# Query features in an attention-and-experts kernel: from turned exponentials to a second, transposed projection

## The chip, the cores and the metric

The kernel runs on one core of one Trainium2 chip. The metric is the device time of one execution in microseconds (us), shown as the median of several runs. Beside it stands the profile of one execution, whose span is the time from the first to the last instruction on the core.

## The reference

Two stages follow each other. The first is linear attention with random features over 4 batches, 8 heads, 576 positions and 64 channels, with 128 features:

```
def phi(x):
    proj = np.einsum('bhsd,md->bhsm', x, omega)
    sq = np.sum(x * x, axis=-1, keepdims=True) / 2.0
    h = proj - sq
    h = h - np.max(h, axis=-1, keepdims=True)
    return np.exp(h) / np.sqrt(m)
q_p, k_p = phi(q * scale), phi(k * scale)
kv = np.einsum('bhsm,bhsd->bhmd', k_p, v)
z = np.sum(k_p, axis=2)
num = np.einsum('bhsm,bhmd->bhsd', q_p, kv)
den = np.einsum('bhsm,bhm->bhs', q_p, z)[..., None] + 1e-06
out = num / den
```

The second takes the 2304 tokens of 512 channels through 8 experts (hidden size 1024, relu), each expert's result weighted by a gate that is normalized eight times over rows and columns, and adds them up.

## The kernel before

**The attention** is cut into 36 jobs, 18 for keys and 18 for queries. A job is 128 positions (or two times 64 left over) of eight head-and-position groups. The list `jobs` begins with keys, then alternates keys and queries, and ends with queries alone. A function `tick(j)` writes out, for every j, what is done for job j (`now`), for the job before it (`prev` in the new code, `job(j - 1)` in the old), for `job(j - 2)` and for the job two ahead (`far`). The order of the instructions of each engine is fixed as written (they are pinned), so an engine that waits holds up everything written behind it.

A job goes through these steps. `transposes` (L442, tile `tp`) turns the inputs with four matmuls against the identity; `transposed_copy` brings them to SBUF as `th`, by ScalarE for keys (L450) and by VectorE for queries (L452). `projections` (L462, tile `pp`) multiplies by `omega`, eight matmuls into two PSUM banks; each takes 64 rows of the array, the bank of g = 0 the upper rows and that of g = 1 the lower ones, and each f32 matmul stands as two records in the trace. `maxima` (L472) takes the largest feature of each position. `shifts` adds the three parts of the shift (L477, tile `cn`) and adds it to the first bank (L479, tile `ex`). `exps` takes the exponential: of the first bank in one instruction (L488), of the second in four, with the shift as bias (L492).

For a key job, `keys_by_values` (L499, tile `kv`) multiplies the features by the values. For a query job, the next tick's `query_transposes` (L559, tile `qp`) turns the eight 128x128 blocks of features with TensorE, `query_copy` (L566, tile `qt`) brings them to SBUF by ScalarE, and a tick later `numerators` (L583, tile `np`) multiplies them by the key-value sums; `quotients` (L598 to L602) divides, and `token_transposes` (L618, tile `xp`) turns the tokens for the experts.

Six PSUM banks are shared by `pp`, `tp`, `qp`, `np`, `xp` and the gate's logits (`lp`, L194); two more hold the key-value sums. Between the steps of the attention, generators advance the experts' preparation: the tokens of three chunks are added and subtracted in pairs by GpSimd (L116), rounded by ScalarE (L120), their low parts taken by VectorE or GpSimd (L125), and the pieces are written to DRAM (`xd`) from four buffers (`xs`). Behind the attention TensorE runs the experts in fp32r, in pieces of 384 columns (L730) and 256 columns (L854), in an order made by a planner.

Of the kernel before, what the change touches and what calls it, by code (L numbers as in the profile page):

```python
# [9 lines left out]
F32 = mybir.dt.float32  # L10
F32R = mybir.dt.float32r
AF = mybir.ActivationFunctionType
ALU = mybir.AluOpType
AX = mybir.AxisListType


def raw(ap):

    return ap.bitcast(F32)
# [3 lines left out]
def moe_attention_kernel(  # L23
# [23 lines left out]
    nc = tc.nc  # L47
    B, H, S, D = q.shape
# [4 lines left out]
    P = 128  # L53
# [26 lines left out]
    def bank(name):  # L80
        return ps[0].tile([P, 512], F32, tag="b", name=name)


    ident = const.tile([P, P], F32, name="ident")
# [238 lines left out]
    sc = sc_cm.__enter__()  # L323
# [4 lines left out]
    sc.tile([P, 1, D], F32, name="om2")  # L328
    oms = sc.tile([P, 2, D], F32, name="oms")
    omt = sc.tile([P, M], F32, name="omt")  # L330

    def busy(n):

        wp_ = bank("warm")
        for i in range(n):
            nc.tensor.transpose(wp_[:, i % 4 * P : (i % 4 + 1) * P], ident, ident)

    def prepare_omega():

        nc.scalar.mul(oms, om.to_broadcast([P, 2, D]), 1.0 / math.sqrt(math.sqrt(D)))  # L340
        om_ps = bank("om_ps")
        nc.tensor.transpose(om_ps[:, :P], oms.rearrange("p a d -> p (a d)"), ident)
        nc.scalar.copy(omt, om_ps[:, :M])

    GC = P // KD
    wgs = sc.tile([P, KD, GC], F32, name="wgs")
# [82 lines left out]
    def slots(key, hh, g):  # L429

        if key[0] == "r":
            return [(2 * i + g, 0) for i in range(4)]
        return [(4 * hh + i, g) for i in range(4)]
# [11 lines left out]
    def transposed_copy(jb):  # L445

        which, tp = jb[0], tps.pop(jb)
        th = sc.tile([P, 4, P], F32, tag="th", bufs=2, name="th")
        if which == "k":
            nc.scalar.copy(th.rearrange("p a s -> p (a s)"), tp)  # L450
        else:
            nc.vector.tensor_copy(th.rearrange("p a s -> p (a s)"), tp)  # L452
        ths[jb] = th

    def projections(jb):

        th = ths.pop(jb)
        pp = [bank("pp") for _ in range(2)]
        for i in range(4):
            for g in range(2):  # L460
                r = slice(g * D, (g + 1) * D)
                nc.tensor.matmul(pp[g][:, i * M : (i + 1) * M], lhsT=th[r, i], rhs=omt[r], start=True, stop=True)  # L462
        p3s[jb] = [p.rearrange("p (h m) -> p h m", h=4) for p in pp]

    def shift_of(jb):

        which, key, hh = jb[:3]
        return sqt[which, key].rearrange("p h j t -> p (h j) t")[:, 8 * hh : 8 * hh + 8]

    def maxima(jb, g):  # L470

        nc.vector.tensor_reduce(shift_of(jb)[:, g::2, 1], p3s[jb][g], axis=AX.X, op=ALU.max, negate=True)  # L472

    def shifts(jb):

        cn = sc.tile([P, 8], F32, tag="cn", bufs=4, name="cn")
        nc.vector.tensor_reduce(cn, shift_of(jb), axis=AX.X, op=ALU.add)  # L477
        ex = [sc.tile([P, 4, M], F32, tag="ex", bufs=6, name="ex") for _ in range(2)]
        nc.vector.tensor_tensor(  # L479
            ex[0], p3s[jb][0], cn[:, 0::2].unsqueeze(2).to_broadcast([P, 4, M]), op=ALU.add  # L480
        )
        cns[jb], exs[jb] = cn, ex

    def exps(jb, g):

        ex = exs[jb][g]
        if g == 0:
            nc.scalar.activation(ex, ex, AF.Exp)  # L488
            return
        c4 = cns.pop(jb)[:, 1::2]  # L490
        for i in range(4):
            nc.scalar.activation(ex[:, i, :], p3s[jb][1][:, i, :], AF.Exp, bias=c4[:, i : i + 1])  # L492

    tps, ths, p3s, cns, exs, qts, nums = {}, {}, {}, {}, {}, {}, {}

    def kv_mm(b, h, r, ex, rhs, z, start, stop):

# [51 lines left out]
    closing = []  # L549
    xts = {}  # L550

    def query_transposes(jb):

        ex = exs.pop(jb)
        tps = []
        for g in (1, 0):
            tp = bank("qp")
            for i in range(4):
                nc.tensor.transpose(tp[:, i * P : (i + 1) * P], ex[g][:, i, :], ident)  # L559
            tps.append((g, tp))  # L560
        return tps

    def query_copy(jb, g, tp):

        t = sc.tile([P, 4, P], F32, tag="qt", bufs=4, name="qt")
        nc.scalar.copy(t.rearrange("p a s -> p (a s)"), tp)  # L566
        qts[jb, g] = t

    def numerators(jb):

        key, hh = jb[1:3]
        shared = key[0] == "r"
        n3s = []
        for g in range(2):
            nps = bank("np")
            n3 = nps[:, : 4 * (D + 1)].rearrange("p (h d) -> p h d", h=4)
            n3s.append(n3)
            qt = qts.pop((jb, g))
            for i, (h, j) in enumerate(slots(key, hh, g)):
                for a in range(2):  # L580
                    r = slice(a * SR, (a + 1) * SR)
                    kv = kvs[2 * key[1] + a if shared else key[0]]
                    nc.tensor.matmul(  # L583
                        n3[r, i, :], lhsT=qt[:, i, r], rhs=kv[:, h], start=True, stop=True
                    )
        nums[jb] = n3s
# [372 lines left out]
    jobs = []  # L959
# [46 lines left out]
    def go_on():  # L1006
        for it in list(extra):
            if next(it, it) is it:
                extra.remove(it)

    def tick(j):

        def job(n, which=None):
            return jobs[n] if 0 <= n < len(jobs) and which in (None, jobs[n][0]) else None

        now, nxt, far = job(j), job(j + 1), job(j + 2)
        if j < 0:
            transposes(nxt)
            transposed_copy(nxt)
            busy(3)  # L1020
            _, w, key = sq_todo.pop(0)
            squares(w, key)
            it = sq_halves.pop(0)
            next(it)
            next(it)
            transposes(far)
            transposed_copy(far)
            ensure_squares(0)
            return
        closed = []  # L1030

        def close():
            while closing:
                closed.append(closing.pop(0))
                kv_copy(*closed[-1])

        close()
        if now:
            projections(now)
            maxima(now, 0)  # L1040
        if j >= 3:
            ensure_squares(j)
        if far:
            transposes(far)
        shared = None
        if job(j - 1, "k") and job(j - 1)[1][0] == "r":
            shared = keys_by_values(job(j - 1))
            next(shared)
            close()
        it = None  # L1050
        if j >= 0 and sq_halves:
            it = sq_halves.pop(0)
            next(it)
        if 1 <= j < 3:
            ensure_squares(j - (j < 2))
        if job(j - 1, "q"):
            for t in query_transposes(job(j - 1)):
                query_copy(job(j - 1), *t)
        if now:
            if not nxt:  # L1060
                go_on()
            maxima(now, 1)
            shifts(now)
        for b, g in closed:
            kv_add(b, g)
        if far:
            transposed_copy(far)
        if now:
            if it:
                next(it)  # L1070
            exps(now, 1)
        go_on()
        for xt, i, t in turned[: 1 if j < 28 else None]:
            turned.pop(0)
            token_copy(token_transposes(xt, i, t), t)
        if now:
            exps(now, 0)
        for it in leftover:
            next(it, None)
        leftover.clear()  # L1080
        if job(j - 2, "q"):
            numerators(job(j - 2))
        if shared:
            leftover.append(shared)
        elif job(j - 1, "k"):
            it = keys_by_values(job(j - 1))
            next(it)
            leftover.append(it)
        if job(j - 2, "q"):
            quotients(job(j - 2))  # L1090
        if nxt:
            go_on()
# [4 lines left out]
    busy(16)  # L1097
    ensure_loads(0)
    prepare_omega()
    for i in range(-1, len(jobs)):  # L1100
        if i == 7:
            stage(0, 1)
            prepare_gate()
        if i == 12:
            it = first_splits()
            next(it)
            extra.append(it)
        if i == 32:
            stage(0, 2)
        tick(i)  # L1110
        ensure_loads(i + 1)
    z = len(jobs)
    numerators(jobs[z - 2])
    for g, tp in query_transposes(jobs[z - 1]):
        query_copy(jobs[z - 1], g, tp)
    go_on()
    xpss = [token_transposes(*it) for it in turned[:2]]
    quotients(jobs[z - 2])
# [5 lines left out]
    xt, i, t = turned.pop(0)  # L1124
# [4 lines left out]
    xt, i, t = turned.pop(0)  # L1129
# [48 lines left out]
    for s, (u, n) in enumerate(steps):  # L1178
        c = n // (CT // 2)
# [27 lines left out]
        for k, i in enumerate(ORDER):  # L1207
# [3 lines left out]
            if k < ((5, 5, 4) if s > 2 else (3, 4, 3))[n % 3] and todo:  # L1211
                pc = todo.pop(0)
                first(*pc)
                j = ORDER.index(pc[2])
# [44 lines left out]
```

## Time and profile before

| what | value |
|---|---|
| median of 3 runs | 1576.74 us (1575.73 to 1577.12) |
| profiled execution, its own time | 1575.99 us |
| its span | 1574.2 us |
| TensorE clock granted | 1.00 of full speed in every slice |
| attention | to about 146.8 us, when the first experts' matmul starts |

The busy time of TensorE is modelled and overlaps from one matmul to the next, so the distance from the start of one group of records to the start of the next says more of what a group costs than its busy time.

### The profile page before, as it was taken

What the parts mean: (1) busy time and instruction counts of PE and PEld (TensorE: products, weight loads), DVE (VectorE), ACT (ScalarE), POOL (GpSimd) and SP (SyncE); (2) the same over time, 40 slices, a digit from 0 to 9 for tenths busy, and PEclk for the clock granted to TensorE, in tenths of its full rate; (3) what the DMA queues carried; (4) which work ended last, traced back from release to release, by engine and by line L of the source; (5) the groups of instructions that cost most, each with busy time, mean ns of one, the idle gap of its engine ahead of it and who ended that gap; (6) DMA issues with size and microseconds to landing.
All of it is one profiled execution on the core that took longest, in us unless ns stands there. A gap on an engine that the chain in (4) does not pass through costs nothing.

```text
span 1574.2 us, 31256 instructions
## 1 busy us (share of the span) xinstructions
PE 1561.7 (99%) x12295; PEld 1535.4 (98%) x12295; DVE 1361.5 (86%) x2573; ACT 766.2 (49%) x1388; POOL 277.1 (18%) x285
## 2 busy tenths in 40 slices
PE   9999999999999999999999999999999999999999
PEld 8887999999999999999999999999999999999998
DVE  7999989898888898888789898889888888989775
ACT  8998654444443444444444443444443444444341
POOL 6665211111010111111011111111110111110000
PEclk9999999999999999999999999999999999999999
DMA  9546866645666666656666666656566666656562
GB/s 227 139 148 259 332 249 223 229 173 214 210 222 215 225 197 216 222 176 216 214 221 212 225 208 212 217 185 225 195 219 212 216 217 208 225 185 212 182 230 92
DMA packets 105730, 330.81 MB, mean 210 GB/s; under 512 B 14704, under 2 KB 43888, under 8 KB 105584
## 3 DMA queue, kind: packets, MB, share of 16 engines
q1 hardware_dynamic: 105296, 328.55, 61.8%
q8 instruction: 98, 1.61, 0.4%
q14 instruction: 48, 0.39, 0.1%
q10 hardware_dynamic: 288, 0.26, 0.0%
HBM read 307.54 MB, written 21.23 MB: 209 GB/s over the span
## 4 chain that ended last, share of the span: by engine, by line
PE 91%; DVE 3%; DMA 3%; ACT 1%; SPq 1%; POOL 1%; issue 0%; DVEq 0%; POOLq 0%; ACTq 0%
PE hx L730 25%; PE x L854 25%; PE hz L730 19%; PE z L854 19%; PE p L938 1%; PE pp L462 1%; DMA xd<-xs 1%; DVE sqs L472 1%; DMA oa<-xd 1%; DMA xs<-xd 1%; DMA k<-in_k_dram 1%; DVE xs L125 0%; PE tp L442 0%; PE np L583 0%; PE kv L499 0%
## 5 line engine op out<-in xcount | busy, mean ns | idle before, releaser
L730 PE MATMUL hx<-xs,wh 128*128 128x384 f32 x1528 | 367.0, 335 | 1.1 <-ACT hn L745 0.8
L730 PE MATMUL hz<-xs,wh 128*128 128x384 f32 x1144 | 282.1, 336 | 0.3 <-DMA xs<-xd 0.3
L730 PEld LDWEIGHTS hx<-xs,wh 128*128 128x128 f32 x1528 | 265.4, 188 | 2.8 <-ACT xs L120 1.4
L235 POOL TENSOR_TENSOR st<-st 128x512 f32<-128x512 f32 x75 | 117.6, 1568 | 613.6 <-DVE wl L269 611.3
L828 ACT ACTIVATE bh<-hr 128x512 fp32r<-128x512 f32 x141 | 89.1, 632 | 237.6 <-PE x L854 230.1
L730 PEld LDWEIGHTS hz<-xs,wh 128*128 128x128 f32 x1144 | 199.8, 188 | 1.5 <-DVE out L888 0.9
L730 PE MATMUL hx<-xs,wl 128*128 128x384 f32 x764 | 200.1, 335 | 0.0
L888 DVE SCALAR_TENSOR_TENSOR out<-x,prob,out 128x256 f32<-128x256 f32 x324 | 153.7, 477 | 52.3 <-PE x L854 50.4
L268 ACT CAST wh<-st 128x512 fp32r<-128x512 f32 x172 | 103.5, 620 | 103.4 <-PE hx L730 52.1
L730 PE MATMUL hz<-xs,wl 128*128 128x384 f32 x572 | 151.8, 335 | 0.0
L825 DVE TENSOR_TENSOR sl<-sm,sh 128x512 fp32r<-128x512 f32 x141 | 112.7, 799 | 44.2 <-ACT sh L823 38.4
L823 ACT CAST sh<-sm 128x512 fp32r<-128x512 f32 x141 | 87.7, 622 | 106.3 <-PE z L854 82.0
L730 PEld LDWEIGHTS hx<-xs,wl 128*128 128x128 f32 x764 | 137.4, 188 | 0.0
L269 DVE TENSOR_TENSOR wl<-st,wh 128x512 fp32r<-128x512 f32 x172 | 123.1, 725 | 9.9 <-ACT wh L268 9.9
L783 DVE SCALAR_TENSOR_TENSOR sm<-hr,sm 128x256 f32<-128x256 f32 x282 | 124.6, 442 | 3.0
L809 ACT CAST sh<-sm 128x512 fp32r<-128x512 f32 x140 | 87.1, 622 | 71.3 <-PE x L854 68.5
L854 PE MATMUL z<-wh,sh 128*128 128x256 f32 x564 | 115.9, 280 | 0.6 <-ACT sh L809 0.5
L854 PE MATMUL x<-wl,sh 128*128 128x256 f32 x564 | 114.5, 280 | 0.0
L854 PE MATMUL z<-wl,sh 128*128 128x256 f32 x564 | 113.9, 280 | 0.0
L854 PE MATMUL x<-wh,sl 128*128 128x256 f32 x564 | 113.6, 279 | 0.0
L791 ACT ACTIVATE ah<-hr 128x256 fp32r<-128x256 f32 x141 | 58.9, 418 | 109.8 <-PE x L854 95.5
L854 PE MATMUL x<-wh,sh 128*128 128x256 f32 x564 | 112.3, 279 | 0.0
(194 smaller groups left out, 3555.6 us busy)
## 6 DMA issues: line engine op xcount, KB each, us to landing
xs<-xd SPq DMA_DIRECT2D x327, 768.0 KB, 4.5
st<-in_moe_w_dram SPq DMA_DIRECT2D x66, 512.0 KB, 4.9
xd<-xs SPq DMA_DIRECT2D x21, 768.0 KB, 5.3
v<-in_v_dram SPq DMA_DIRECT2D x8, 512.0 KB, 7.0
q<-in_q_dram SPq DMA_DIRECT2D x8, 512.0 KB, 7.1
k<-in_k_dram SPq DMA_DIRECT2D x7, 512.0 KB, 7.3
out_dram<-out SPq DMA_DIRECT2D x18, 128.0 KB, 3.9
oa<-xd SPq DMA_DIRECT2D x2, 768.0 KB, 8.9
```

Source lines behind the costliest of these rows:

```text
L235: nc.gpsimd.tensor_tensor(o, a, b, op=op)
L268: nc.scalar.copy(hi, o)
L269: nc.vector.tensor_tensor(lo, o, raw(hi), op=ALU.subtract)
L730: nc.tensor.matmul(pb, lhsT=a[:, k, g * P : (g + 1) * P], rhs=x[:, b, k, :], start=i in (1, 5, 2) and j == 0, stop=j == len(prods) - 1, sk ...
L783: nc.vector.scalar_tensor_tensor(o, in0=a, scalar=0.0, in1=b, op0=ALU.max, op1=op)
L791: nc.scalar.activation(ah, a11, AF.Relu)
L809: nc.scalar.copy(sh, sm)
L823: nc.scalar.copy(sh, sm)
L825: nc.vector.tensor_tensor(sl, sm, raw(sh), op=ALU.subtract)
L828: nc.scalar.activation(bh, a[:, 1:], AF.Relu)
L854: nc.tensor.matmul(pb, lhsT=ops[s][i][a][:, f], rhs=wt[u, 2, i][b][:, f], start=bool(start) and j == 0, stop=j == len(prods) - 1, skip_gro ...
L888: nc.vector.scalar_tensor_tensor(o, in0=pb, scalar=p, in1=o, op0=ALU.mult, op1=ALU.add)
```

## The change

For query jobs the features are no longer turned after the exponential. The projection is computed a second time with the operands exchanged, so that features stand on the partitions and positions along the free axis. The shift, one number for each position, then has to be added along the free axis. For that, `shifts` writes it in two parts into a zeroed 128x128 tile `cnw` (rounded to fp32r, and what the rounding left), `shifts_turned` turns that tile with one matmul against the identity and copies it to `ct`, and `query_features` adds it to the second projection with eight fp32r matmuls against constant tiles `pick` of ones and zeros. `query_exps` takes the exponential straight from PSUM into `qt`. The first projection stays, since the maximum is taken from it; the add to the first bank and the two forms of the exponential fall away for query jobs, and so do the turning and the copy. Buffers: `th` grows from two to four, `qt` shares the six buffers of `ex`, and constants are prepared at the start.

```
+    wide = [sc.tile([P, P], F32R, name=f"cw{i}") for i in range(2)]
+    turnedc = [sc.tile([P, P], F32R, name=f"ct{i}") for i in range(2)]
+    for t in wide:
+        nc.gpsimd.memset(raw(t), 0.0)
...
+    def prepare_pick():
+        for i in range(4):
+            t = sc.tile([P, 1], F32, tag="cn", bufs=4, name="pk")
+            nc.vector.tensor_reduce(t, ident[:, i::32], axis=AX.X, op=ALU.add)
+            nc.vector.tensor_copy(pick[:, i], t.to_broadcast([P, P]))
...
-        th = sc.tile([P, 4, P], F32, tag="th", bufs=2, name="th")
+        th = sc.tile([P, 4, P], F32, tag="th", bufs=4, name="th")
...
 def shifts(jb):
+        if jb[0] == "q":
+            cnw = wide[len(cnws) % 2]
+            cnws.append(cnw)
+            c8 = sc.tile([P, 8], F32, tag="cn", bufs=4, name="cq")
+            nc.vector.tensor_reduce(c8, shift_of(jb), axis=AX.X, op=ALU.add)
+            parts = cnw.rearrange("p (g a c) -> p a c g", g=2, a=2)[:, :, :4, :]
+            c8 = c8.rearrange("p (i g) -> p i g", g=2)
+            nc.vector.tensor_copy(parts[:, 0], c8)
+            nc.vector.tensor_tensor(parts[:, 1], c8, raw(parts[:, 0]), op=ALU.subtract)
+            return
 def exps(jb, g):
+        if jb[0] == "q":
+            return
...
+    def shifts_turned(jb):
+        cp = p3s[jb][0].rearrange("p h m -> p (h m)")[:, :P]
+        nc.tensor.transpose(cp, raw(cnws[-1]), ident)
+        ct = turnedc[len(cnws) % 2]
+        nc.vector.tensor_copy(ct, cp)
...
+    def query_features(jb):
+        th, ct = ths.pop(jb), cts.pop(jb)
+        qp = [bank("qp") for _ in range(2)]
+        rows = [slice(g * D, (g + 1) * D) for g in range(2)]
+        for g, r in enumerate(rows):
+            nc.tensor.matmul(
+                qp[g][:, :], lhsT=omt[r], rhs=th[r].rearrange("p a s -> p (a s)"), start=True, stop=False,
+                skip_group_check=True,
+            )
+        for i in range(4):
+            for g, r in enumerate(rows):
+                nc.tensor.matmul(
+                    qp[g][:, i * P : (i + 1) * P], lhsT=pick[r, i],
+                    rhs=ct[r], start=False, stop=i == 3, skip_group_check=True,
+                )
+    def query_exps(jb):
+        for g, qp in enumerate(qps.pop(jb)):
+            t = sc.tile([P, 4, P], F32, tag="ex", bufs=6, name="qt")
+            nc.scalar.activation(t.rearrange("p a s -> p (a s)"), qp, AF.Exp)
...
 def tick(j):
         close()
+        prev = job(j - 1, "q")
+        if prev:
+            shifts_turned(prev)
         if now:
             projections(now)
...
-        if job(j - 1, "q"):
-            for t in query_transposes(job(j - 1)):
-                query_copy(job(j - 1), *t)
+        if prev:
+            query_features(prev)
...
             exps(now, 1)
+            exps(now, 0)
+        if prev:
+            query_exps(prev)
         go_on()
```

Of the lines left out, the exponential of the first bank moves ahead of the token copies for key jobs too, and the end of the loop does the new steps for the last job.

## Rows read from the trace of the kernel before

**Rows 1.** The page's chain that ended last: shares of the span by engine.

```profile
PE 91%; DVE 3%; DMA 3%; ACT 1%; SPq 1%; POOL 1%; issue 0%; DVEq 0%; POOLq 0%; ACTq 0%
```

**Rows 2.** Busy time by stretch: length, then each engine's, granted clock, DMA.

```profile
28.60:64.80 36.20, 36.20 (x593) 32.52 (x589) 32.80 (x77) 32.55 (x81) 21.36 (x42) 1.00 0.83 205
64.80:85.60 20.80, 20.30 (x339) 17.03 (x338) 17.78 (x43) 20.80 (x52) 13.99 (x25) 1.00 0.01 2
85.60:125.40 39.80, 38.42 (x598) 33.30 (x592) 38.47 (x84) 34.83 (x86) 28.42 (x46) 1.00 0.52 170
125.40:146.80 21.40, 20.11 (x310) 15.64 (x306) 20.34 (x51) 19.24 (x41) 18.90 (x11) 1.00 0.58 229
```

**Rows 3.** The chain that ended last, in order of time: start, us, what.

```profile
68.62 0.94 ACT ex L492 x3
...
91.59 1.21 DVE sqs L472 x2
...
138.66 1.79 POOL xs L125
...
152.33 0.97 PE hx L730 x4
```

**Rows 4.** Timeline of TensorE: start, us to its last end, instructions.

```profile
30.14 1.46 PE L462 MATMUL pp<-omt,th 64*128 64x128 f32 x16
31.53 0.66 PE L442 MATMUL tp<-ident,q 128*128 128x128 f32 x4
32.12 1.15 PE L583 MATMUL np<-kvs,qt 128*64 128x65 f32 x32
33.10 1.10 PE L499 MATMUL kv<-v,ex 128*64 128x65 f32 x32
34.13 1.16 PE L462 MATMUL pp<-omt,th 64*128 64x128 f32 x16
35.23 0.66 PE L442 MATMUL tp<-ident,k 128*128 128x128 f32 x4
35.72 1.04 PE L559 MATMUL qp<-ident,ex 128*128 128x128 f32 x8
36.69 1.46 PE L462 MATMUL pp<-omt,th 64*128 64x128 f32 x16
```

**Rows 5.** The same timeline, the last of the 22 places where TensorE waits.

```profile
144.67 0.63 PE L618 MATMUL xp<-ident,xt 128*128 128x128 f32 x4 [0.79 <-DVE xt L602]
```

**Rows 6.** The same timeline in two narrow windows of the gate's logits.

```profile
79.92 0.51 PE L194 MATMUL lp<-xf,wgs 128*32 128x384 f32 x4
...
80.25 0.51 PE L194 MATMUL lp<-xf,wgs 128*32 128x384 f32 x4
```

**Rows 7.** The chain in the experts, fp32r matmuls of 256 columns.

```profile
1509.31 0.71 PE x L854 x6
```

**Rows 8.** Weight loads of an fp32r and an f32 matmul, groups by line.

```profile
L730 PEld LDWEIGHTS hx<-xs,wh 128*128 128x128 f32 x1528 | 265.4, 188 | 2.8 <-ACT xs L120 1.4
...
L462 PEld LDWEIGHTS pp<-omt,th 64*128 64x128 f32 x576 | 38.6, 187 | 6.4 <-ACT qt L566 2.5 <-issue 1.2 <-DVE ex L479 0.6
```

**Rows 9.** VectorE by line, 28.6 to 147 us: busy, mean ns, idle before.

```profile
L479 DVE TENSOR_TENSOR ex<-pp,cn 128x512 f32<-128x512 f32 x29 | 20.0, 691 | 1.6
L602 DVE TENSOR_TENSOR xt<-np,rd 128x256 f32<-128x256 f32 x36 | 13.6, 418 | 0.6
...
L599 DVE RECIPROCAL rd<-rd 128x8 f32<-128x8 f32 x18 | 3.6, 203 | 0.6
```

**Rows 10.** VectorE by line, 0 to 28 us.

```profile
L411 DVE TENSOR_REDUCE sqs<-sq 128x8 f32<-128x512 f32 x2 | 1.4, 683 | 6.6 <-ACT sq L409 6.6
```

**Rows 11.** ScalarE by line, 28.6 to 147 us.

```profile
L492 ACT ACTIVATE ex<-pp,cn 128x128 f32<-128x128 f32 x116 | 34.7, 425 | 3.8 <-DVE cn L477 3.5
L488 ACT ACTIVATE ex<-ex 128x512 f32<-128x512 f32 x30 | 21.4, 714 | 0.0
L566 ACT COPY qt<-qp 128x512 f32<-128x512 f32 x36 | 20.1, 617 | 5.6 <-PE qp L559 5.5
```

More of the change, by code (lines that the diff above doesn't have):

```diff
@@ L343, in prepare_omega @@
         nc.scalar.copy(omt, om_ps[:, :M])
+    pick = sc.tile([P, 4, P], F32R, name="pick")
+    def prepare_pick():
[3 more added lines that the diff above has]
+            nc.vector.tensor_copy(pick[:, i], t.to_broadcast([P, P]))
     GC = P // KD
@@ L455, in projections @@
     def projections(jb):
-        th = ths.pop(jb)
+        th = ths[jb] if jb[0] == "q" else ths.pop(jb)
         pp = [bank("pp") for _ in range(2)]
@@ L492, in exps @@
             nc.scalar.activation(ex[:, i, :], p3s[jb][1][:, i, :], AF.Exp, bias=c4[:, i : i + 1])
-    tps, ths, p3s, cns, exs, qts, nums = {}, {}, {}, {}, {}, {}, {}
+    tps, ths, p3s, cns, exs, qts, nums, cts, qps = {}, {}, {}, {}, {}, {}, {}, {}, {}
     def kv_mm(b, h, r, ex, rhs, z, start, stop):
@@ L550, in moe_attention_kernel @@
     xts = {}
[L552 to L567, printed above, removed]
+    cnws = []
+    def shifts_turned(jb):
[3 more added lines that the diff above has]
+        nc.vector.tensor_copy(ct, cp)
+        cts[jb] = ct
+        p3s.pop(jb)
+    def query_features(jb):
[13 more added lines that the diff above has]
+                )
+        qps[jb] = qp
+    def query_exps(jb):
+        for g, qp in enumerate(qps.pop(jb)):
+            t = sc.tile([P, 4, P], F32, tag="ex", bufs=6, name="qt")
+            nc.scalar.activation(t.rearrange("p a s -> p (a s)"), qp, AF.Exp)
+            qts[jb, g] = t
     def numerators(jb):
@@ L1075, in tick @@
             token_copy(token_transposes(xt, i, t), t)
-        if now:
-            exps(now, 0)
         for it in leftover:
@@ L1099, in moe_attention_kernel @@
     prepare_omega()
+    prepare_pick()
     for i in range(-1, len(jobs)):
@@ L1112, in moe_attention_kernel @@
     z = len(jobs)
+    shifts_turned(jobs[z - 1])
     numerators(jobs[z - 2])
-    for g, tp in query_transposes(jobs[z - 1]):
-        query_copy(jobs[z - 1], g, tp)
+    query_features(jobs[z - 1])
+    query_exps(jobs[z - 1])
     go_on()
```

## The prediction

> **What bounds the kernel now.** I read the chain of waits of the whole span first: it is TensorE for 91% of its length [rows 1]. The experts are a stream in which TensorE hardly stops, and the change does not touch it, so what counts is how much later or earlier the experts begin, at 146.8 us. The attention before that point has no single limit. In four stretches with different limits, between 28.6 us (the first query features are turned at 29.2) and 146.8 us, TensorE, VectorE and ScalarE are all busy for about nine tenths [rows 2]. The chain in order of time says which is last where: TensorE alone up to 64 us, then pieces of ScalarE (one of them is a key or query job's exponentials), from 85 us VectorE (the maxima), from about 126 us GpSimd's sums for the second chunk's tokens, which are written to DRAM before the experts' next piece can start [rows 3].
>
> A busy share close to 1 on TensorE proves little, because its ends are modelled. So I went to its timeline and took the distance from start to start as the price of a group. One pair of a key and a query tick runs from 30.14 to 36.69 us, 6.55 us. In it the projections cost 1.09 us (34.13 to 35.23), the four turns of the inputs 0.49 us when other 128-row matmuls follow and 0.59 us when matmuls of another shape follow, the eight turns of query features 0.97 us, the numerators 0.98 us, the key-value products 1.03 us [rows 4]. The projections at 30.14 take 1.39 us, 0.30 us more than those at 34.13: a wait for a PSUM bank. Adding up what every group costs beyond the shortest of its kind between 28.6 and 146.8 us, I find 22 places over 0.1 us, the first at 30.14 us, the last at 144.67 us (the wait of one query job's token for VectorE), 8.8 us together [rows 4, 5]: 1.9 us in the first stretch, 1.1, 4.3 and 1.4 us in the other three. So of 118.2 us TensorE really works about 109, and it has under 0.5 us of slack for each of the 18 query jobs.
>
> **What the change takes away and adds.** *ScalarE.* A query job loses four exponentials of 128 columns (0.43 us each), one of 512 (0.71) and two copies (0.62 each), and gets two exponentials of 512 columns from PSUM, which I price like the one it loses, 0.71 each [rows 11]. That is 3.65 us against 1.42, so 2.2 us of busy time less for each job, 40 us in all; since instructions overlap by about 0.1 us the real relief is nearer 30. It is large, but it only counts where ScalarE is last.
>
> *VectorE.* It loses the add to the first bank, 0.69 us. It gets two operations on 128x8, for which I take 0.20 us each from the reciprocal of that size, and the copy of the turned shift out of PSUM, 128x128, between 0.20 us (128x8) and 0.42 us (128x256); I take 0.28 [rows 9]. Sum 0.68, so no change; between 0.1 us better and 0.15 worse a job. The copy stands first in VectorE's tick, ahead of the maxima, which wait for the projections anyway. At the start VectorE gets four sums and four 128x128 copies, 4 x (0.20 + 0.28) = 1.9 us, in the 6.6 us in which it waits for ScalarE's squares [rows 10]; without that cover it would cost these 1.9 us once. The two clearings on GpSimd at the start lie in the same wait.
>
> *TensorE.* A query job loses the eight turns, 0.97 us. It gets three things:
>
> - One turn of the shift tile between the key-value products and the projections. The smallest distance between two groups of different shape is what 0.59 and 0.49 us differ by on top of one record's 0.11 us (0.97 us hold eight), so about 0.20 us. And the input turns are now followed by 64-row matmuls, 0.59 in place of 0.49 us: 0.10 more [rows 4].
> - The second projection: two f32 matmuls of 512 columns, one on each half of the rows. In the logits, f32 records of 384 columns on different parts of the array start together and the next ones 0.33 us later [rows 6]; at 512 columns that is 0.44 us. The first projections show sixteen records in 1.09 us, 0.07 each, where the input turns need 0.11 each, so the two halves of the rows run together too [rows 4]. Each f32 matmul is two records, so 2 x 0.44 = 0.88 us.
> - Eight fp32r matmuls of 128 columns, in four pairs. No row has this form. From above: f32 pairs of 128 columns in the projections, (1.09 - 0.20) / 8 = 0.11 us a pair, and fp32r matmuls of 256 columns at 0.71 / 6 = 0.12 us [rows 4, 7]. From below: the numerators' 32 records in 0.98 us, 0.06 us a pair, with half the weights and half the columns [rows 4]. The weights to load are those of the projections, so I take 0.11: 0.44 us, and 0.24 as the lower end. The group's end adds the 0.20 us that a group with a change of shape shows.
>
> Sum: 0.20 + 0.10 + 0.88 + 0.44 + 0.20 - 0.97 = +0.85 us a query job, with 0.65 as the lower end; 18 jobs make 15.3 us (11.7). If the two halves did not run together, it would be 0.88 + 0.44 more a job.
>
> The step between 0.49 and 0.59 us shows that a change of shape costs about 0.1 us on TensorE [rows 4]. The Trainium skill says it in TensorEngine Tiling, section Key Properties: changing the tiling mode, not only the tile, drains the engine. By that rule the two changes of shape that the new steps add to a tick are paid every time, and this trace agrees with its 0.59 against 0.49 us; without it the sum would be some 18 x 0.2 = 3.6 us lower.
>
> **What of it reaches the end.** Stretch by stretch, with the query jobs turned in each:
>
> - 28.6 to 64.8 us, six jobs. TensorE is last here, so all of 6 x 0.85 = 5.1 us counts, less the 1.9 us of waits for a bank, which the longer features give VectorE time to clear: +3.2.
> - 64.8 to 85.6 us, two jobs. 1.7 us more, of which 1.1 us fall into the present waits, since ScalarE is relieved: +0.6.
> - 85.6 to 125.4 us, six jobs. 5.1 us more against 4.3 us of waits. VectorE, busy for 38.5 of 39.8 us, is not relieved, so some waits stay; a sixth of them: +1.5.
> - 125.4 to 146.8 us, four jobs. 3.4 us more against 1.4 us of waits, +2.0 on TensorE. But GpSimd, busy 18.9 of 21.4 us, sets when the experts' next piece can start, and it is not slowed once its tokens are there. I take half: +1.0.
>
> Together +6.3 us. The profiled execution took 1575.99 us for a span of 1574.2; its median stands 0.75 us above it. 1575.99 + 6.3 = 1582.3, and with the 0.75 us, 1583 us for the median. A difference under 0.2%, 3.2 us, I call no change, which is about what a measurement of this kernel can tell.
>
> **Rivals.**
>
> *Hidden (0.15, about 1579 us).* TensorE's work lies under VectorE and GpSimd from 85.6 us on, which cost what they did, and the fp32r pairs take 0.06 us. For it speaks that VectorE and GpSimd end the chain there [rows 3]; against it that TensorE is nearly as full. Then 3.2 + 0.6 us remain, less 0.20 x 8 = 1.6: +2.2, so 1579.
>
> The weight loads of fp32r and f32 matmuls stand with 188 and 187 ns in the rows, so fp32r shows no quicker load [rows 8]. The Trainium skill, TensorE: Matmul & The Clock Gate, section on weight-path performance modes, says that a fast weight load is on where there are 128 weights and the type is not FP32. If fp32r counted as such a type, the pairs would be near the lower end of 0.06 us and this rival would hold; the equal loads in this trace speak against it.
>
> *Dear (0.17, 1591 us and more).* The fp32r matmuls at 128 columns run no quicker than f32, two records' time for a pair: 0.22 us, 0.44 us more a job, 8 us more in all, 1591. Against it speaks 0.12 us for 256 columns [rows 7]; nothing narrower is there. If the halves of the rows did not run together, 18 x 1.32 = 24 us would come on top of the forecast, some 1607; the rows of the projections speak against that [rows 4], so I give it 0.04 of the 0.17.
>
> *ScalarE was the limit (0.09, 1573 us).* From 64 us on TensorE waits for others often enough that its new work costs nothing, and ScalarE's relief shortens the chain: three jobs' share of the ScalarE chain around 64 to 85 us, 3 x 1.6 = 4.8 us, and 1.8 us at the end, where the last job's exponentials and copies stand in a row. Against that stands +3.2 in the first stretch: -3.4, so 1573. It decides once TensorE's new work is under the slack of about 0.5 us a job; I have 0.85, with 0.65 as the lower end. The ScalarE pieces in the chain speak for it [rows 3], the 109 us of real work against it.
>
> **How the numbers follow.** The forecast, 1580 to 1588 us, gets 0.59. Slower by over 0.2% is forecast and dear case together, 0.76; no change 0.15; faster 0.09. The range from 1577 to 1592 us leaves out the faster case, part of the hidden one and the upper end of the dear one, about 2 in 10.
>
> **What will show it.** In the profile after, a query job's features should take 1.5 us from their first matmul to the next group, and a pair of ticks near 40 us 7.1 us in place of 6.55; the projections after a key tick should lose their 0.30 us; ScalarE should be busy for some 40 us less; the first experts' matmul should start near 153 us. The prediction is wrong if the features take under 1.2 us, if the waits at 85 to 125 us grow (VectorE's copy of the shift late, and TensorE's features with the token turns and numerators behind it), or if the experts' stream itself comes out in another order and length.

## The result and the profile after

The changed kernel takes 1592.24 us (median of 4 runs, 1591.86 to 1592.63) against 1576.24 us before, measured beside it: 16.0 us slower, a ratio of 1.0102 with a 95% interval of 1.0084 to 1.0119. The forecast was slower by 6.3 us, 1583 us, with a range to 1592. The side was right, the size was not, and the time lies just outside the range. One execution among all those below (in the run on ScalarE's order) took 2188.67 us at a mean granted clock of 0.655 and is left out of its run's time.

The chain that ended last is still TensorE's, by engine on the page of the kernel after:

```profile
PE 94%; DVE 4%; ACT 1%; DMA 1%; issue 1%; POOL 0%; DVEq 0%; ACTq 0%; POOLq 0%
```

The first experts' matmul starts at 164.7 us in place of 146.8, 17.8 us later; the rest of the kernel gives back 1.8 us. Busy time by stretch, cut at the same steps of the work as [rows 2] (length, busy time and count of PE, PEld, DVE, ACT, POOL, granted clock, DMA share, GB/s):

```profile
29.50:69.70 40.20, 39.42 (x621) 31.85 (x619) 33.24 (x89) 25.51 (x56) 21.78 (x42) 1.00 0.72 176
69.70:91.40 21.70, 21.43 (x354) 16.96 (x350) 17.99 (x45) 17.70 (x40) 12.67 (x24) 1.00 0.01 2
91.40:137.30 45.90, 42.67 (x625) 34.57 (x623) 41.04 (x98) 25.54 (x54) 27.28 (x47) 0.96 0.48 160
137.30:164.70 27.40, 22.71 (x327) 16.29 (x326) 24.40 (x58) 13.44 (x23) 18.58 (x11) 1.00 0.42 169
```

The stretches are 4.0, 0.9, 6.1 and 6.0 us longer than those of [rows 2]; 0.9 us stand ahead of them. Forecast were 3.2, 0.6, 1.5 and 1.0. So the error lies behind 91 us, and there ScalarE is idle for long (busy for only 25.5 of 45.9 us and 13.4 of 27.4) and TensorE idle too, 3 and 5 us by its generous busy time.

The timeline of TensorE shows a pair of ticks as in [rows 4]:

```profile
35.40 0.33 PE L582 MATMUL pp<-ident,cw 128*128 128x128 f32 x1
35.66 1.16 PE L475 MATMUL pp<-omt,th 64*128 64x128 f32 x16
36.75 0.66 PE L455 MATMUL tp<-ident,k 128*128 128x128 f32 x4
37.33 1.13 PE L594 MATMUL qp<-th,omt 64*128 64x512 f32 x4
37.90 0.96 PE L600 MATMUL qp<-ct,pick 64*128 64x128 f32 x8
38.69 1.11 PE L475 MATMUL pp<-omt,th 64*128 64x128 f32 x16
39.73 0.66 PE L455 MATMUL tp<-ident,q 128*128 128x128 f32 x4
40.69 1.17 PE L627 MATMUL np<-kvs,qt 128*64 128x65 f32 x32 [0.30 <-ACT qt L610]
41.70 1.10 PE L524 MATMUL kv<-v,ex 128*64 128x65 f32 x32
42.73 0.33 PE L582 MATMUL pp<-ident,cw 128*128 128x128 f32 x1
```

The features take 37.33 to 38.69, 1.36 us with the fp32r matmuls (forecast 1.52), the turn of the shift 0.26 us (forecast 0.20). The projections at 38.69 have lost their wait. The new one stands in front of the numerators: 0.96 us from the input turns to them, where 0.59 would do.

VectorE by line, 28 to 165 us (busy, mean ns, idle before), beside [rows 9]:

```profile
L497 DVE TENSOR_TENSOR cw<-cq,cw 128x8 fp32r<-128x8 f32 x17 | 8.1, 478 | 0.6
L496 DVE CAST cw<-cq 128x8 fp32r<-128x8 f32 x17 | 6.6, 390 | 0.6
L584 DVE CAST ct<-pp 128x128 fp32r<-128x128 f32 x18 | 5.1, 281 | 0.2 <-PE pp L582 0.2
```

The copy of the turned shift costs the 0.28 us that were forecast. The two operations on 128x8, forecast at 0.20 us, have means of 0.48 and 0.39. By instruction, the shortest take 0.17 us, fourteen and eleven of the 18 take at most 0.18, and the longest take 1.75 and 1.61 us. What such a one waits for is seen by laying VectorE's timeline beside GpSimd's. VectorE:

```profile
94.96 1.61 DVE L496 CAST cw<-cq 128x8 fp32r<-128x8 f32 x1
96.60 1.18 DVE L497 TENSOR_TENSOR cw<-cq,cw 128x8 fp32r<-128x8 f32 x1
...
140.07 0.80 DVE L496 CAST cw<-cq 128x8 fp32r<-128x8 f32 x1
140.90 1.75 DVE L497 TENSOR_TENSOR cw<-cq,cw 128x8 fp32r<-128x8 f32 x1
```

GpSimd in the same windows:

```profile
94.72 1.82 POOL L116 TENSOR_TENSOR xf<-xf 128x768 f32<-128x768 f32 x1
...
140.76 1.85 POOL L116 TENSOR_TENSOR v<-xf,v 128x768 f32<-128x768 f32 x1
```

The rounding copy starts at 94.96, while GpSimd subtracts tokens from 94.72 on, and ends at 96.57, when GpSimd is done at 96.54. At 140.90 the subtraction starts 0.14 us behind a GpSimd instruction of 1.85 us and ends with it, at 142.65 against 142.61. All eleven that take longer than 0.18 us are like this: each starts while a GpSimd instruction is under way and ends 0.03 to 0.04 us behind one. The table of waits names none of this, since in the trace it is part of the instruction's own duration. What stands behind them then waits in the usual way, among it the turn of the shift on TensorE and, at its head, the next job's projections:

```profile
97.84 0.33 PE L582 MATMUL pp<-ident,cw 128*128 128x128 f32 x1 [2.08 <-DVE cw L497]
...
156.13 0.33 PE L582 MATMUL pp<-ident,cw 128*128 128x128 f32 x1 [1.44 <-DVE cw L497]
```

### The profile page after: what moved, and what is told of

Its sections match the earlier page's. It is cut to its first block, busy times and chain, and to the rows that moved or that the text cites. A ratio compares the mean times of both kernels' runs of the same rounds, so it can differ in the third digit from the quotient of the medians.

```text
span 1590.2 us, 31369 instructions
## 1 busy us (share of the span) xinstructions
PE 1572.3 (99%) x12385; PEld 1537.8 (97%) x12385; DVE 1369.8 (86%) x2617; ACT 739.2 (46%) x1298; POOL 277.6 (17%) x287
## 3 DMA queue, kind: packets, MB, share of 16 engines
q8 instruction: 98, 1.61, 0.4%
## 4 chain that ended last, share of the span: by engine, by line
PE 94%; DVE 4%; ACT 1%; DMA 1%; issue 1%; POOL 0%; DVEq 0%; ACTq 0%; POOLq 0%
PE hx L774 25%; PE x L898 25%; PE hz L774 19%; PE z L898 19%; PE pp L475 1%; DVE sqs L485 1%; PE p L982 1%; PE np L627 1%; PE kv L524 1%; DMA oa<-xd 1%; PE tp L455 1%; PE qp L594 1%; PE xp L662 0%; ACT ex L517 0%; DVE xt L646 0%
## 5 line engine op out<-in xcount | busy, mean ns | idle before, releaser
L898 PE MATMUL z<-wh,sl 128*128 128x256 f32 x564 | 112.3, 279 | 0.0
```

Source lines behind the costliest of these rows:

```text
L898: nc.tensor.matmul(pb, lhsT=ops[s][i][a][:, f], rhs=wt[u, 2, i][b][:, f], start=bool(start) and j == 0, stop=j == len(prods) - 1, skip_gro ...
```

## The experiments

Theory 1, formed from these rows: the two small instructions, with all their operands in SBUF, wait for GpSimd's instructions, and about half of the loss comes from that; the rest is TensorE's work at about the forecast price. Theory 2, its rival: TensorE's 15 us of new work reach the end in full, and VectorE's long instructions lie beside that.

**The shift in PSUM.** One line, which takes one SBUF operand away from each of the two instructions and leaves count, size and order as they are:

```
-            c8 = sc.tile([P, 8], F32, tag="cn", bufs=4, name="cq")
+            c8 = p3s[jb][0].rearrange("p h m -> p (h m)")[:, 2 * P : 2 * P + 8]
```

> The changed kernel, but the summed shift c8 stands in PSUM (in the bank whose maxima are done) and no longer in SBUF, so that the two small VectorE instructions that write the shift's high and low parts have at most one operand in SBUF. Theory 1 (these two instructions wait for GpSimd, and about 9 of the 16 us come from that): both stay under 0.25 us in every job, the first experts' matmul starts near 156 us in place of 164.7, and the time falls by 7 to 9 us, to 1583 to 1585. Theory 2 (the 15 us of TensorE's new work reach the end in full, and VectorE's waits lie beside them): the instructions are short too, but the time falls by under 3 us, to 1589 or more.

1585.13 us, a ratio to the kernel before of 1.0054 (1.0039 to 1.0069), 7.1 us less than the change. All 36 instructions now last about 0.17 us, by the view of each line (shortest, median and longest ns, first and last start):

```profile
L497 DVE TENSOR_TENSOR cw<-pp,cw x18: 171/172/175, 27.5 to 148.9; 128x8 fp32r<-128x8 f32 x18
```

They are short beside GpSimd too. VectorE:

```profile
137.13 0.17 DVE L496 CAST cw<-pp 128x8 fp32r<-128x8 f32 x1
```

GpSimd at the same time:

```profile
135.97 1.83 POOL L116 TENSOR_TENSOR v<-xf 128x768 f32<-128x768 f32 x1
```

The first experts' matmul starts at 157.8 us. Theory 1 is confirmed, with its size at the lower end (7.1 us of the 7 to 9 expected, and a start at 157.8 where about 156 was expected); theory 2 falls.

**The two small instructions alone, in the kernel before.**

```
+        if jb[0] == "q":
+            s2 = small[len(exs) % 2]
+            nc.vector.tensor_copy(s2[:, :8], cn)
+            nc.vector.tensor_tensor(s2[:, 8:], cn, raw(s2[:, :8]), op=ALU.subtract)
         nc.vector.tensor_tensor(
             ex[0], p3s[jb][0], cn[:, 0::2].unsqueeze(2).to_broadcast([P, 4, M]), op=ALU.add
```

> The kernel before, and in each query job's shift two more VectorE instructions on 128x8, a rounding copy and a subtraction from SBUF to SBUF, into tiles that nobody reads. TensorE's work is as before. Theory 1: some of them take 1 to 1.8 us where GpSimd works, and the time rises by 4 to 9 us. Theory 2: it rises by under 3 us.

1589.91 us, 13.4 us more than before (1.0087, 1.0072 to 1.0102). That is more than theory 1 expected, and no run takes the surplus apart. TensorE's clock has a part in it that the expectation did not have: in the profiled execution TensorE stood for 1.98 and 2.75 us behind the long instructions, and the granted clock was 0.50 from 140 to 142 and from 154 to 156 us. Groups by line:

```profile
L483 DVE TENSOR_TENSOR sm<-cn,sm 128x8 fp32r<-128x8 f32 x18 | 8.7, 484 | 0.6
L482 DVE CAST sm<-cn 128x8 fp32r<-128x8 f32 x18 | 8.4, 467 | 0.8 <-DVE cn L478 0.2
```

**The same two, reading PSUM.**

```
+            low8 = p3s[jb][0].rearrange("p h m -> p (h m)")[:, :8]
-            nc.vector.tensor_copy(s2[:, :8], cn)
-            nc.vector.tensor_tensor(s2[:, 8:], cn, raw(s2[:, :8]), op=ALU.subtract)
+            nc.vector.tensor_copy(s2[:, :8], low8)
+            nc.vector.tensor_tensor(s2[:, 8:], low8, raw(s2[:, :8]), op=ALU.subtract)
```

> The kernel before with the two small VectorE instructions added in each query job, as in the run that took 13.4 us more, but both read a PSUM bank in place of SBUF (the numbers go nowhere). Same count, same size, same place in the order. Theory 1 (VectorE and GpSimd shut each other out of SBUF): every one takes under 0.25 us and the time rises by 1 to 4 us. Rival (two more links in VectorE's chain cost that much wherever their operands stand): it rises by 10 us or more.

1576.86 us against 1576.67: a ratio of 1.0004 (0.9994 to 1.0013), no difference. The 36 instructions take 0.16 us each:

```profile
L484 DVE TENSOR_TENSOR sm<-pp,sm 128x8 fp32r<-128x8 f32 x18 | 3.0, 166 | 0.6
L483 DVE CAST sm<-pp 128x8 fp32r<-128x8 f32 x18 | 2.8, 156 | 0.2 <-issue 0.2
```

Same instructions, same place; only what they read, and where, differs, and 13.2 us go with it. (They no longer need the sum `cn`, but in the run before VectorE stood idle in front of them for only 0.6 and 0.8 us in all.) The time rises by even less than the 1 to 4 us expected: the 5.8 us that they are busy are hidden, presumably in VectorE's gaps.

**TensorE's work alone.** The kernel before, with its eight turns of query features made twice, 0.87 us of TensorE more a job:

```
-            for i in range(4):
+            for i in (0, 1, 2, 3, 0, 1, 2, 3):
                 nc.tensor.transpose(tp[:, i * P : (i + 1) * P], ex[g][:, i, :], ident)
```

> The kernel before with the eight turns of query features made twice into the same place: 0.87 us more of TensorE a query job, nearly what the change adds, and nothing more on VectorE, ScalarE and GpSimd. Theory 1 (the forecast's covers hold): plus 5 to 8 us. Theory 2: plus 13 to 16 us.

1583.98 us, 7.5 us more than before (1.0048, 1.0033 to 1.0063), inside theory 1's 5 to 8 and far from theory 2's 13 to 16. Of 15.7 us of new work on TensorE a little under half reaches the end.

**The turn behind the projections.**

```
-        if prev:
-            shifts_turned(prev)
         if now:
             projections(now)
+        if prev:
+            shifts_turned(prev)
+        if now:
             maxima(now, 0)
```

> The changed kernel with the turn of the shift behind the projections in TensorE's order, not ahead of them; c8 in SBUF as in the change. Theory 1a (what counts is the time that VectorE itself loses in its two locked instructions): the waits of the turn become shorter, but the time falls by under 2.5 us. Theory 1b (what counts is that the turn, waiting for them, holds up the projections behind it on TensorE): it falls by 4 to 7 us, as much as with c8 in PSUM.

1592.17 us, as the change (1592.24). The wait of the turn for the small instructions shrinks from 3.9 to 1.0 us in the table of TensorE's waits (waited for: us in total, times, longest). The changed kernel:

```profile
PE pp L582 <- DVE cw L497: 3.9, 3, 2.1
```

With the turn behind the projections:

```profile
PE pp L582 <- DVE cw L497: 1.0, 1, 1.0
```

Nothing is gained, though: the waits in that table add up to 8.9 us before the edit and 10.0 after it, so they have only moved. That speaks for theory 1a, by which the time that VectorE loses is what counts. It does not exclude a small share of theory 1b, since the next run shows that the later place of the turn has a price of its own, about 1.4 us.

> Both: c8 in PSUM and the turn behind the projections. The turn then waits for nothing in either place; it follows 64-row matmuls and is followed by the input turns of its own shape, so one change of shape a tick falls away, about 0.1 to 0.15 us on TensorE. All theories: 0 to 2 us below 1585.1 us. If it comes out under 1580 us, the place of the turn holds up more than the trace shows.

With c8 in PSUM as well: 1586.52 us, 1.4 us slower than with the turn in front. All theories missed that. The table of VectorE's waits suggests the copy of the turned shift, which stands at the head of VectorE's tick:

```profile
DVE ct L584 <- PE pp L582: 7.8, 13, 1.5
```

It now waits for a turn that comes after the projections, 7.8 us in place of 0.4. The maxima behind it wait less for that, 3.8 us in place of 9.1; together the two wait 2.1 us more.

**ScalarE's order.**

```
-            exps(now, 1)
-            exps(now, 0)
         if prev:
             query_exps(prev)
+        if now:
+            exps(now, 1)
+            exps(now, 0)
```

> The changed kernel with the query job's exponentials ahead of the present job's in ScalarE's order, not behind them. In the trace after, numerators wait about 0.35 us for these exponentials in some ten ticks. Both theories: the time falls by 2 to 3.5 us, and these waits go; if TensorE then waits for the keys' exponentials in place of them, it falls by under 1 us. The two small VectorE instructions stay as long as they were.

1591.93 us (the middle one of 1591.87, 1591.93 and 1593.10), no change. The wait in front of the numerators goes, and one in front of the key-value products takes its place, as the last clause had it (timeline of TensorE):

```profile
40.51 1.15 PE L627 MATMUL np<-kvs,qt 128*64 128x65 f32 x32
41.83 1.15 PE L524 MATMUL kv<-v,ex 128*64 128x65 f32 x32 [0.17 <-ACT ex L513]
```

**Without the eight fp32r matmuls**, with c8 in PSUM; the features lack their shift.

```
-        for i in range(4):
-            for g, r in enumerate(rows):
-                nc.tensor.matmul(
-                    qp[g][:, i * P : (i + 1) * P], lhsT=pick[r, i],
-                    rhs=ct[r], start=False, stop=i == 3, skip_group_check=True,
-                )
```

> The kernel with c8 in PSUM (1585.1 us), without the eight fp32r matmuls that add the shift, so the features lack their shift; the turn of the shift and its copy stay. That takes 0.4 us of TensorE from each query job, 7 to 8 us in all. Theory 1 (about half of TensorE's added work reaches the end, as the doubled turns showed with 7.5 of 15.7 us): the time falls by 3 to 5 us, to 1580 to 1582. Rival (these short matmuls lie in waits that would be there without them): it falls by under 1 us.

1583.47 us, 1.7 us less than with them: between the theories, and with intervals against the kernel before that overlap (1.0028 to 1.0058 here, 1.0039 to 1.0069 with them). The timeline shows where the 0.4 us a job went: the numerators wait 0.78 us for ScalarE where they waited 0.34, and the pair of ticks stays as long (7.36 us against 7.37).

```profile
41.23 1.17 PE L621 MATMUL np<-kvs,qt 128*64 128x65 f32 x32 [0.78 <-ACT qt L604]
```

So in the first stretch something other than TensorE's work closes the pair. The chain of the changed kernel says what, in order of time:

```profile
28.50 1.14 PE pp L475 x16
29.64 1.28 DVE sqs L485 x2
...
31.16 0.75 ACT ex L517 x3
...
32.17 0.64 ACT ex L513
32.82 0.50 ACT qt L610
...
33.36 1.18 PE np L627 x32
34.53 0.93 PE kv L524 x32
...
35.73 1.14 PE pp L475 x16
```

From projections to projections, 7.23 us, it goes through the key job's maxima and exponentials, then the query job's, then the numerators and the key-value products. To test that ring, the products were put ahead of the numerators (c8 in PSUM), so that they lie over the query job's exponentials:

```
-        if job(j - 2, "q"):
-            numerators(job(j - 2))
         if shared:
             leftover.append(shared)
         elif job(j - 1, "k"):
             it = keys_by_values(job(j - 1))
             next(it)
             leftover.append(it)
+        if job(j - 2, "q"):
+            numerators(job(j - 2))
```

> The kernel with c8 in PSUM (1585.1 us), with the key-value products ahead of the numerators in TensorE's order. In the chain of the changed kernel near 30 us a ring closes: projections, maxima, the key job's exponentials, the query job's exponentials behind them, numerators, key-value products. Theory A (this ring, not TensorE's work, sets the pair of ticks in the first stretch): the numerators' wait goes, since the products lie over the query job's exponentials, the pair near 40 us falls from 7.3 to about 7.0 us, and the time falls by 1.5 to 3.5 us, to 1582 to 1583.5. Theory B (TensorE's work sets it): the time falls by under 1 us.

1584.17 us, 1.0 us less (1.0048 to the kernel before, 1.0031 to 1.0064). The pair falls from 7.37 us with c8 in PSUM alone to 6.94 us (35.57 to 42.51), without a wait between the input turns and the products:

```profile
35.57 0.33 PE L582 MATMUL pp<-ident,cw 128*128 128x128 f32 x1
...
39.90 0.66 PE L455 MATMUL tp<-ident,q 128*128 128x128 f32 x4
40.49 1.15 PE L524 MATMUL kv<-v,ex 128*64 128x65 f32 x32
41.47 1.10 PE L627 MATMUL np<-kvs,qt 128*64 128x65 f32 x32
42.51 0.33 PE L582 MATMUL pp<-ident,cw 128*128 128x128 f32 x1
```

The ring is there, as theory A had it, but at the end it is worth about 1.0 us, the bound of theory B and less than theory A's 1.5. The intervals of the two runs against the kernel before overlap (1.0039 to 1.0069 with c8 in PSUM alone), so this figure is rough.

Both edits together, the products first and no fp32r matmuls:

> The same order and also without the eight fp32r matmuls, so that the features lack their shift. Theory A (the ring hid what these matmuls cost when they were left out, 1.7 us of 7 to 8): with the ring open they are worth 3 us or more, so 3 us or more below the run with the products first. Theory B: under 2 us below it, as with the ring closed.

1581.36 us, 2.8 us less than with the fp32r matmuls in the same order. Just short of theory A's 3 us and above theory B's 2: with the ring open these matmuls seem to cost more than the 1.7 us seen before, though the two figures are only 1.1 us apart.

No version here that computes the same beats the kernel before; the best one, with c8 in PSUM and the products first, stays 7.4 us behind it.

## Why the prediction was wrong

**The step that failed** is VectorE's: "two operations on 128x8, for which I take 0.20 us each from the reciprocal of that size", and with it the sum "0.68, so no change", with 0.15 us a job as the worse end. Their own time is right, 0.17 us. But the forecast put their wait for GpSimd at nothing, without a reason: with all operands in SBUF they wait for a GpSimd instruction that is under way (this wait is called the lock below), and GpSimd works for 27 of 46 us in the third stretch and 19 of 27 in the last. The 36 instructions took 15.4 us in place of the 6.3 that 0.175 us each make. The run with c8 in PSUM shows the value at the end, 7.1 us; the pair of runs on the kernel before, with the same instructions reading SBUF or PSUM, shows that it is where they read and not their number, size or place (13.4 and 0.2 us).

The Trainium skill has the rule, in SBUF — State Buffer, section Who interferes with whom: VectorE and GpSimd share one pair of ports, an instruction of VectorE with two SBUF inputs, or a copy in a two-port mode, is fully shut out while GpSimd holds it, and one with at most one SBUF input outside these modes is not. The traces agree: 1.61 and 1.75 us beside GpSimd, 0.16 to 0.17 from PSUM. Whether the rounding copy runs in such a mode no trace shows by itself, only that it is shut out like the subtraction.

The profile before could have told it. [rows 2] shows GpSimd busy for 28 and 19 us in the last two stretches, and the forecast used that only for the chain of the tokens. VectorE's timeline shows the lock itself, in an instruction that also takes two inputs from SBUF (L125): 0.94 us where GpSimd stands idle, 1.90 us where it starts 0.20 us behind a GpSimd instruction. VectorE before:

```profile
134.38 1.90 DVE L125 TENSOR_TENSOR xs<-xf,xs 128x768 fp32r<-128x768 f32 x1
...
136.45 0.20 DVE L599 RECIPROCAL rd<-rd 128x8 f32<-128x8 f32 x1
...
146.85 0.94 DVE L125 TENSOR_TENSOR xs<-xf,xs 128x768 fp32r<-128x768 f32 x1
```

GpSimd before:

```profile
134.18 4.48 POOL L287 TENSOR_TENSOR st<-st 128x512 f32<-128x512 f32 x3
```

The reciprocal (L599) is the row from which the price was taken. It takes 0.20 us even while GpSimd works: it has the right size, but it isn't held up, so it could not stand for the two new instructions.

**Right: TensorE's work.** +0.85 us a job was forecast; the features take 1.36 us where 1.52 was said, the turn of the shift 0.26 where 0.20 was, which with 0.09 more for the input turns and 0.97 less for the old turns makes +0.74. The two row halves run together, and the fp32r pairs are not dear. What of it reaches the end was forecast at 6.3 us; the doubled turns, with nearly the same work, give 7.5, and the change without its lock 8.6 (1585.13 against 1576.53). Without the lock the stretches are 4.0, 1.1, 2.7 and 2.1 us longer, against 3.2, 0.6, 1.5 and 1.0 forecast: each more, about twice as much from the second on, but small beside the 6.1 and 6.0 us with the lock.

**Too good: the first stretch.** "5.1 us counts, less the 1.9 us of waits for a bank" left out a new wait. The projections lost theirs, as forecast, but the query job's exponentials now stand behind the key job's on ScalarE, where the copies stood ahead, and the numerators wait for them. The pair near 40 us took 7.33 us, not 7.1, and 6.94 with the order changed. At the end that is about 1.0 us.

**The sum.** Of the 16.0 us, 7.1 are the lock (1592.24 - 1585.13, with what the fall of TensorE's clock behind it cost), about 1.0 the ring (1585.13 - 1584.17), and 7.4 remain (1584.17 - 1576.76). These I put down to TensorE's new work, since the doubled turns alone cost 7.5; no run that computes the same takes that work away. The 0.5 us left are the difference between two medians of the kernel before (1576.24 and 1576.76).

**The rivals.** The dear case had the time (1591) for another reason: its pairs were to take 0.22 us each and take about 0.10, so its near hit is luck. That ScalarE was the limit is excluded: its relief came (82 us busy in the four stretches in place of 107, less than the 40 us forecast), it sits idle for up to 3 or 4 us at a time, and the time rose. That VectorE and GpSimd would hide TensorE's work in the later stretches was the wrong way round: together they added to it. Of the signs of being wrong, the growing waits behind 85 us came, but by the two small instructions and not by the copy of the shift, which was named.

## What to carry to other kernels

A small instruction isn't priced by its size alone: ask of each new VectorE instruction where its operands stand and what GpSimd does then, since a wait for a port shows up as a long duration and not as a wait. A row for an instruction of the same size isn't a price either if it is of another kind: here the reciprocal, in SBUF too, isn't held up by GpSimd, while the cast and the subtraction are. If an instruction can read PSUM, even scratch space in a bank that is done, that costs nothing here and saved 7 us. And where several engines are nine tenths busy, relief of one can be worth little: ScalarE's 25 us bought nothing that any run here shows.

## What the runs showed of the hardware

TensorE's clock fell during one of the waits of the changed kernel. Ahead of it TensorE had stood for 2.08 us, waiting for the small subtraction; the granted clock then was 0.55 over the next 3.8 us (about 0.5, the lower level of 1.2 GHz, in most of them) and 1.00 again after that. The stretches:

```profile
94.00:98.00 4.00, 1.92 (x57) 1.69 (x53) 3.82 (x6) 2.21 (x4) 3.75 (x6) 1.00 0.25 101
98.00:101.80 3.80, 3.80 (x23) 2.96 (x24) 3.14 (x7) 0.58 (x2) 3.40 (x7) 0.55 0.43 160
101.80:106.00 4.20, 4.20 (x68) 3.37 (x66) 3.84 (x6) 4.20 (x11) 1.02 (x1) 1.00 0.99 326
```

The projections in it took 1.97 us in place of 1.09 and the input turns 1.04 in place of 0.59, some 1.3 us of the third stretch in that execution. With the turn behind the projections the clock stayed at 1.00 in these stretches, and the time was the same. That suggests a follower of the lost time more than a cause of its own; but the later place of the turn cost 1.4 us by itself with c8 in PSUM, which could hide as much, so what the fall is worth at the end stays open.

Not expected either: two busy instructions more for each query job on VectorE, 5.8 us in all, cost nothing that can be measured on an engine that was busy for nine tenths, as long as they read PSUM and don't wait for GpSimd.
